# Linear attention feeding a two-layer MLP: four output tiles of block 0 held open beside batch 1's attention, and the steps of batches 2 and 3 moved

## The chip, the cores and the metric

The kernel runs on one core of a Trainium2 chip. The engines of the core are TensorE (PE in the profile, its weight loads PEld), VectorE (DVE), ScalarE (ACT), GpSimd (POOL) and SyncE (SP, which here only issues DMAs). The metric is the time of one execution on the device in microseconds, the median of several runs. Times inside a profile are microseconds from the start of its span.

## The reference

For 8 batches and 8 heads, with 576 tokens of 64 numbers, attention without a softmax is followed by a norm over each head; the heads are put side by side to 4608 tokens of 512 numbers, which go through two matrix products with a leaky rectifier between them.

```
kv  = einsum("bhsd,bhse->bhde", k, v)
o   = einsum("bhsd,bhde->bhse", q, kv)
o   = o / sqrt(mean(o*o, -1) + 1e-6) * g_norm
x   = o.transpose(0, 2, 1, 3).reshape(4608, 512)
h   = x @ w_in                                   # 4608 x 2048
g   = max(h, 0) + alpha * min(h, 0)
out = g @ w_out                                  # 4608 x 512, float32
```

## The kernel before

**Blocks and groups.** The 4608 tokens are cut into 9 blocks of 512 (`w`), so that blocks and batches of 576 tokens drift apart. For a block, the 2048 hidden numbers are 16 groups of 128 (`g`). `m1_group` (L480) makes one group: four matmuls of 512 columns over the four 128-row pieces of the input (L465), into one PSUM bank; ACT makes `m_sb` (L472), the rectified negative, and DVE puts both together to `gt` (L474), 128 x 512 in half precision. `y_mm` (L487) is one matmul of the second product: 128 tokens (tile `a`, four per block) by 512 outputs, with group `g` added in; 16 of them fill one output tile. `y_out` (L492) copies it out of PSUM on ACT or DVE, and SP issues two DMAs (L505). In the loop at L631 the output tiles of block `w - 1` are made beside the hidden groups of block `w`: in step `g`, after the group, four `y_mm` of tile `g // 4`.

**Attention.** Loads (L93) go through POOL's queue, two DMAs for each of q, k, v of a batch, from float32 into half precision. `regroup` (L105) copies q and k into another order, on DVE or POOL. Batches 0 and 1 (`NB_PE = 2`) are done with transposes on PE: `step_t` (L210) makes transposed q of a pair of heads, `step_kv` (L228) the product of k and v (20 matmuls, then a masking multiply on DVE, L242), `step_ot` (L262) the output of a pair for one block and its square, `ssq_mm` (L284) the sum of squares over a head by a matmul, with Ln and Exp on ACT, and `norm` (L295) the scaled input `xt` on DVE. The last 64 columns of batches 0 and 1 that fall in block 2 are the tail (L340, L352).

From batch 2 on, q is transposed by a DMA that SP issues (`transpose_q`, L376), and the attention goes by tiles of 128 tokens in four parts: `tile_a` (L384) product of q and kv into a bank and its square on ACT; `tile_b` (L397) the sum over each head on DVE (L399); `tile_c` (L405) Ln and Exp on ACT and the scale `rg` on POOL (L411); `tile_d` (L418) the scaled row `xrow` on DVE (L420) and one or two DMA transposes into `xm` (L425), the input of a block from block 2 on. `phase_steps(w)` (L431) lists for each step of block `w - 1` what is done for block `w`: a tile's `b` and `c` come one step after its `a`, its `d` two steps after.

**Order.** The order of the instructions on PE, ACT, DVE, POOL and SP is the program's: an instruction that waits holds those behind it on its engine. PSUM has eight banks: three for hidden groups (pool `psh`, tag `h`, taken in turn), one each for `y` and `s`, and `o0`, `o1`, `o2`.

**Around the change.** After block 0's groups (L579), three output tiles of block 0 (`ys`, L587) stay open while batch 1's attention runs; `ahead(g0, g1)` (L593) puts their `y_mm` of some groups between its steps, and L624 copies them out. The fourth tile is made in block 1's loop, one `y_mm` in each step (L638). In that loop the q of batch 2 is regrouped on DVE and transposed after step 1 (L655). After step 3 a one-element copy on POOL, `gate` (L662), waits for that transpose; behind it POOL issues the six loads of batch 3 (L663), and DVE regroups k of batch 2. After step 9 POOL regroups q and k of batch 3 (L665), and after step 13 SP issues its transpose. In block 2 and later the loads of batch `w + 2` are issued ahead of step 6 (L634). `KV_AT = 5` is the step of block 1 with batch 2's kv; its tiles start in step 7. In block 2, batch 3's kv is in step 0, and tiles start there too.

Of the kernel before, what the change touches and what calls it, by code (L numbers as in the profile page):

```python
# [9 lines left out]
FP32 = mybir.dt.float32  # L10
# [7 lines left out]
def kernel(  # L18
# [11 lines left out]
    nc = tc.nc  # L30
# [27 lines left out]
    ysb_p = ctx.enter_context(tc.tile_pool(name="ysb", bufs=4))  # L58
    ps_h = ctx.enter_context(tc.tile_pool(name="psh", bufs=3, space=bass.MemoryType.PSUM))
    ps_y = ctx.enter_context(tc.tile_pool(name="psy", bufs=1, space=bass.MemoryType.PSUM))  # L60
# [58 lines left out]
    for nm in "qkv":  # L119
        zero_rest(stages[0][nm])  # L120

    ident = const_p.tile([P, P], FP32, name="ident")
    make_identity(nc, ident[:])
    HH = H // 2
    for h0 in (0, HH):
        for nm in "qkv":
            load(0, nm, h0, h0 + HH)

# [204 lines left out]

    KV_AT = 5


# [93 lines left out]
    def phase_steps(w):  # L430
# [7 lines left out]
        steps = []  # L438
        kv_at = 0
        if w == NB_PE:  # L440
            n = NPAIR // JT
            for i in range(n + 1):
                m = [lambda i=i: step_tail_ot(i)] if i < n else []
                m += [lambda i=i: step_tail_ssq(i - 1)] if i > 0 else []
                steps.append(([], [], m))
            kv_at = KV_AT
            steps += [([], [], []) for i in range(KV_AT + 2 - len(steps))]
        for i in range(len(todo) + 2):
# [11 lines left out]

    gts = {}

    def m1_mm(h_ps, w, g, cs, cols=slice(0, W)):
# [15 lines left out]

    def m1_group(w, g, pool=(ps_h, "h")):  # L480
        h_ps = pool[0].tile([P, W], FP32, name="h_ps", tag=pool[1])
        m1_mm(h_ps, w, g, range(NC))
        m1_evac(h_ps, w, g)
# [34 lines left out]

    H_POOL = (ps_h, "h")
    O2 = (ps_o, "o2")  # L520
# [4 lines left out]
    )  # L525
    step_t(0, 0, H_POOL)
    step_t(0, 1, H_POOL, nc.scalar)
    regroup(0, "k", 0, HH)
# [7 lines left out]
    ssq_mm(0, 0)  # L536
    step_t(0, 2, H_POOL)
    step_t(0, 3, H_POOL)
    alpha_ps = ps_h.tile([P, NF], FP32, name="alpha_ps", tag="h")
    nc.tensor.matmul(  # L540
# [18 lines left out]
    half_ssq(0, O2)  # L559
    first = [ps_h.tile([P, W], FP32, name="h_ps", tag="h") for g in range(3)]  # L560
    first += [ps_o.tile([P, W], FP32, name="h_ps", tag=f"o{g}") for g in range(2)]
# [17 lines left out]
    for g in range(5, NF):  # L579
        m1_group(0, g, others.get(g, H_POOL))  # L580
        if g == 12:
            spread_g()

    AHEAD = 3
    ys = [  # L587
        ps_y.tile([P, W], FP32, name="ya", tag="y"),
        ps_o.tile([P, W], FP32, name="yb", tag="o0"),
        ps_o.tile([P, W], FP32, name="yc", tag="o1"),  # L590
    ]

    def ahead(g0, g1):  # L593
        for g in range(g0, g1):
            for a in range(AHEAD):
                y_mm(ys[a], 0, a, g)

    S_POOL = (ps_s, "s")
    regroup(1, "k")
    ahead(0, 4)  # L600
    regroup(1, "q")
    step_t(1, 0, S_POOL)
    step_t(1, 1, H_POOL, nc.scalar)
    step_t(1, 2, H_POOL)
    step_t(1, 3, H_POOL, nc.scalar)
    step_kv(1, pool=O2)
    step_ot(1, 0, S_POOL)
    step_ot(1, 1, H_POOL)
    step_ot(1, 2, H_POOL, nc.vector)
    step_ot(1, 3, H_POOL, nc.vector)  # L610
    ahead(4, 5)
    ssq_mm(1, 0)
    ahead(5, 7)
    ssq_mm(1, 1)
    norm(1, 0)
    ahead(7, 9)
    ssq_mm(1, 2)
    norm(1, 1)
    ahead(9, 11)
    ssq_mm(1, 3)  # L620
    norm(1, 2)
    norm(1, 3)
    ahead(11, NF)
    for a in range(AHEAD):  # L624
        y_out(ys[a], 0, a, nc.vector if a == 1 else None)
# [3 lines left out]

    LOAD_G = 6  # L630
    for w in range(1, NW):  # L631
        steps = phase_steps(w + 1)
        for g in range(NF):
# [4 lines left out]
            if w == 1:  # L638
                a, parts = AHEAD, [g]
            begin, mid, end = steps.pop(0) if steps else ([], [], [])  # L640
# [3 lines left out]
            for f in mid:  # L644
                f()
            if parts[0] == 0:
                pool, tag = ((ps_y, "y"), (ps_s, "s"))[a % 2 if w > 1 else 0]
                y = pool.tile([P, W], FP32, name="y_ps", tag=tag)
            for gg in parts:
                y_mm(y, w - 1, a, gg)  # L650
            if parts[-1] == NF - 1:
                y_out(y, w - 1, a)
            for f in end:
                f()
            if (w, g) == (1, 1):  # L655
                regroup(2, "q")
                transpose_q(2)
            if (w, g) == (1, 3):


                gate = const_p.tile([1, 1], FP16, name="gate")
                nc.gpsimd.tensor_copy(out=gate[:], in_=qtms[2][0:1, 0, 0:1])  # L662
                load_batch(3)  # L663
                regroup(2, "k")
            if g == LOAD_G + 3 and w + 2 < B:  # L665
                regroup_batch(w + 2)
            if g == NF - 3 and w + 2 < B:
                transpose_q(w + 2)
    for a in range(TPW):
        y = ps_h.tile([P, W], FP32, name="y_ps", tag="h")  # L670
        for g in range(NF):
            y_mm(y, NW - 1, a, g)
        y_out(y, NW - 1, a)
# [30 lines left out]
```

## Time and profile before

| what | value |
|---|---|
| median of 6 runs | 304.92 us (304.05 to 306.03) |
| the profiled execution's own time | 304.92 us |
| its span, first to last instruction | 302.9 us |
| PE busy | 284.6 us (94%), 1536 matmuls |
| DVE, ACT, POOL busy | 169.9, 152.9, 97.5 us |
| mean granted clock of PE | 0.987 of full speed |
| DMA queue of POOL (loads) / of SP (outputs, transposes) | 18.35 MB / 16.93 MB |
| block 1's first hidden group starts | 48.34 us |
| block 2's first hidden group starts | 78.32 us |

The page cuts the span into 40 slices and gives the busy share of each engine in tenths, and the clock that PE was granted. A line of the waits names the waiting engine, the tile and line, who released it, then microseconds in total, how often and the longest. A line of the timeline has start and duration, the engine, the line of code, the operation with its output and inputs, and in brackets how long the engine had been idle and who ended that. A matmul's shown duration (0.38 us) is longer than the spacing to the next (0.216 us), since they are pipelined. A DMA issue is listed with the time from issue to landing.

### The profile page before, as it was taken

The numbers are of one execution on the slowest core, as the hardware profiler recorded it, in microseconds if no ns is written. First come the engines' busy times: TensorE is split into PE (matmuls) and PEld (weight loads), VectorE is DVE, ScalarE is ACT, GpSimd is POOL, SyncE is SP. The second block draws the span as 40 slices with busy tenths as digits, with TensorE's granted clock in tenths as the row PEclk, the third lists the DMA queues.
The fourth block names the chain that finished last, engine by engine and source line by source line (L and its number), as shares of the span: only waits on it lengthen the run. The fifth ranks groups of instructions, "written<-read, shape, count | busy, mean of one in ns | idle before, by whom it ended". The sixth has DMA issues, their size and how long they took to land.

```text
span 302.9 us, 4249 instructions
## 1 busy us (share of the span) xinstructions
PE 284.6 (94%) x1536; PEld 137.6 (45%) x1536; DVE 169.9 (56%) x261; ACT 152.9 (50%) x297; POOL 97.5 (32%) x109
## 2 busy tenths in 40 slices
PE   5899999873999999999999999999999999999993
PEld 2554544431554454445544544454445444444441
DVE  5569765873486448545963584459546744344200
ACT  1558367460385448445844574458437644434220
POOL 9823400185047505560566054514002300000000
PEclk9999999998799999999999999999999999999999
DMA  7999999598619972994389739935211411122133
GB/s 95 184 206 202 202 203 229 131 163 126 121 33 128 209 169 45 152 230 98 69 112 214 146 78 123 241 80 89 61 35 37 95 35 37 35 47 54 41 69 69
DMA packets 66068, 35.54 MB, mean 117 GB/s; under 512 B 32752, under 2 KB 61440, under 8 KB 66048
## 3 DMA queue, kind: packets, MB, share of 16 engines
q0 software_dynamic: 29664, 18.35, 43.9%
q1 hardware_dynamic: 36384, 16.93, 26.6%
q8 instruction: 12, 0.20, 0.3%
q14 instruction: 8, 0.07, 0.1%
HBM read 36.71 MB, written 9.44 MB: 152 GB/s over the span
## 4 chain that ended last, share of the span: by engine, by line
PE 74%; DMA 11%; issue 8%; POOL 5%; DVE 0%; ACT 0%; POOLq 0%; ACTq 0%
PE y_ps L487 37%; PE h_ps L465 33%; DMA w_in_sb<-in_moe_w_in_dram 5%; DMA w_out_sb<-in_moe_w_out_dram 4%; DMA kst<-in_k_dram 3%; PE otm_ps L387 2%; PE kv_ps L238 2%; POOL w_in_sb L161 1%; POOL qst L96 1%; POOL vst L100 1%; POOL kst L96 1%; POOL qst L100 1%; POOL kst L100 0%; POOL vst L96 0%; POOL rg L411 0%
## 5 line engine op out<-in xcount | busy, mean ns | idle before, releaser
L474 DVE SCALAR_TENSOR_TENSOR gt<-m_sb,beta_sb,h_ps 128x512 f16<-128x512 f32 x144 | 105.8, 744 | 81.1 <-ACT m_sb L472 80.6
L487 PE MATMUL y_ps<-w_out_sb,gt 128*128 128x512 f16 x528 | 135.4, 380 | 0.0
L472 ACT ACTIVATE m_sb<-h_ps 128x512 f32<-128x512 f32 x144 | 85.5, 597 | 95.0 <-PE h_ps L465 94.4
L465 PE MATMUL h_ps<-xm,w_in_sb 128*128 128x512 f16 x448 | 115.7, 381 | 0.0
L465 PEld LDWEIGHTS <-w_in_sb 128*128 128x128 f16 x584 | 56.2, 99 | 69.6 <-issue 11.3
L487 PEld LDWEIGHTS <-gt 128*128 128x128 f16 x576 | 56.3, 98 | 66.8 <-issue 0.5
L411 POOL TENSOR_TENSOR rg<-ss,g_all 128x512 f32<-128x512 f32 (+1 forms) x30 | 31.3, 1046 | 83.7 <-ACT ss L409 83.7
L465 PE MATMUL h_ps<-xt,w_in_sb 128*128 128x512 f16 (+1 forms) x136 | 32.6, 381 | 7.2 <-DVE gt L474 7.2
L497 ACT COPY y_sb<-y_ps 128x512 f32<-128x512 f32 x33 | 19.2, 582 | 17.4 <-PE y_ps L487 17.1
L399 DVE TENSOR_REDUCE ss<-sqm_sb 128x8 f32<-128x512 f32 (+1 forms) x30 | 20.5, 683 | 9.4 <-ACT sqm_sb L393 9.3
L420 DVE TENSOR_TENSOR xrow<-otm_ps,rg 128x512 f16<-128x512 f32 (+1 forms) x30 | 20.4, 682 | 9.2 <-POOL rg L411 9.2
L393 ACT ACTIVATE sqm_sb<-otm_ps 128x512 f32<-128x512 f32 (+1 forms) x30 | 17.8, 592 | 8.5 <-PE otm_ps L387 8.5
L106 POOL COPY qsb<-qst 128x2560 f16<-128x2560 f16 x5 | 11.6, 2317 | 13.9 <-issue 10.2
L106 POOL COPY ksb<-kst 128x2560 f16<-128x2560 f16 x5 | 11.6, 2322 | 7.4 <-DMA kst<-in_k_dram 7.4
L387 PEld LDWEIGHTS <-qtm 128*128 128x128 f16 x120 | 9.2, 98 | 7.1
L197 PE MATMUL warm_ps<-warm,mask 128*128 128x512 f16 x26 | 8.7, 474 | 3.3 <-DVE eps_t L140 3.3
L387 PE MATMUL otm_ps<-kv_sb,qtm 128*128 128x128 f16 x120 | 11.6, 219 | 0.0
L406 ACT ACTIVATE ss<-ss,eps_t 128x8 f32<-128x8 f32 (+1 forms) x30 | 9.0, 301 | 4.7 <-DVE ss L399 4.6
L238 PE MATMUL kv_ps<-vst,ksb 128*128 128x128 f16 x160 | 10.4, 219 | 0.8 <-DMA vst<-in_v_dram 0.4
L238 PEld LDWEIGHTS <-ksb 128*128 128x128 f16 x160 | 9.5, 98 | 3.6 <-DVE ksb L106 1.7
L242 DVE TENSOR_TENSOR kv_sb<-kv_ps,mask 128x512 f16<-128x512 f32 (+1 forms) x9 | 5.7, 628 | 3.4 <-PE kv_ps L238 3.3
L100 POOL DMA_DIRECT2D vst<-in_v_dram x9 | 6.4, 716 | 3.3 <-DMA w_in_sb<-in_moe_w_in_dram 1.9
(72 smaller groups left out, 124.6 us busy)
## 6 DMA issues: line engine op xcount, KB each, us to landing
out_dram<-y_sb SPq DMA_DIRECT2D x72, 128.0 KB, 2.4
kst<-in_k_dram POOLq DMA_DIRECT2D x7, 320.0 KB, 8.2
qst<-in_q_dram POOLq DMA_DIRECT2D x7, 320.0 KB, 5.0
vst<-in_v_dram POOLq DMA_DIRECT2D x7, 320.0 KB, 10.7
w_in_sb<-in_moe_w_in_dram POOLq DMA_DIRECT2D x4, 512.0 KB, 10.5
w_out_sb<-in_moe_w_out_dram POOLq DMA_DIRECT2D x4, 512.0 KB, 15.5
kst<-in_k_dram POOLq DMA_DIRECT2D x7, 256.0 KB, 9.4
qst<-in_q_dram POOLq DMA_DIRECT2D x7, 256.0 KB, 6.4
```

What stands on the lines that cost most here:

```text
L106: (eng or nc.vector).tensor_copy(out=bufs[b % NBUF][nm][:, :, h0:h1, :].rearrange("p t h d -> p h t d"), in_=stages[b % NBUF][nm][:, h0:h1],)
L238: nc.tensor.matmul(out=kv_ps[:, j - j0, :], lhsT=ks(t), rhs=vs(t), start=(t == 0), stop=(t == NT - 1),)
L387: nc.tensor.matmul(out=ot_ps[:, 2 * j : 2 * j + 2, :], lhsT=qtms[b][:, t * NPAIR + j, :], rhs=kvs[b, j], start=True, stop=True,)
L393: nc.scalar.activation(out=sq[0:n], in_=ot_ps[0:n], func=AF.Square)
L399: nc.vector.tensor_reduce(out=ss[0:n], in_=sq[0:n], op=ALU.add, axis=mybir.AxisListType.X,)
L411: nc.gpsimd.tensor_tensor(out=rg[0:n], in0=ss[0:n].unsqueeze(2).to_broadcast([n, H, D]), in1=g_all[0:n].unsqueeze(1).to_broadcast([n, H, D ...
L420: nc.vector.tensor_mul(out=x[0:n], in0=ot_ps[0:n], in1=rg[0:n])
L465: nc.tensor.matmul(out=h_ps[:, cols], lhsT=w_in_blk(c, g), rhs=xt_of(w, c)[:, cols], start=(c == 0), stop=(c == NC - 1 and cols.stop == W),)
L472: nc.scalar.activation(out=m_sb[:], in_=h_ps[:], func=AF.Relu, scale=-1.0)
L474: nc.vector.scalar_tensor_tensor(out=gt[:], in0=m_sb[:], scalar=beta_sb[:, g : g + 1], in1=h_ps[:], op0=ALU.mult, op1=ALU.add,)
L487: nc.tensor.matmul(out=y[:], lhsT=gts[w, g][:, a * P : (a + 1) * P], rhs=w_out_blk(g), start=(g == 0), stop=(g == NF - 1),)
L497: nc.scalar.copy(out=y_sb[:], in_=y[:])
```

## The change

The three banks for hidden groups get a tag each (`h0`, `h1`, `h2`), and the code names the one that it takes; a counter turns them for the groups that name none. All four output tiles of block 0 are opened before batch 1's attention, in `h2`, `o0`, `o2` and `y`; the fourth runs to group 11 there, and groups 12 to 15 in the first four steps of block 1. Batch 1's attention uses `s`, `o1`, `h0` and `h1`; two pairs of `y_mm` stand around its kv; its fourth output comes later, after the first norm. The q of batch 2 is regrouped and transposed before block 0's outputs are copied out. Behind the gate only q and k of batch 3 are loaded, v after step 9; POOL's regroup moves from step 9 to 13 and the transpose of its q from step 13 to 15. In block 2 the steps for block 3 start two steps later, and kv of batch 3 moves from step 0 to step 3. At the start, the first half of batch 0's q is loaded ahead of the identity matrix.

```diff
+    HH = H // 2
+    load(0, "q", 0, HH)
     ident = const_p.tile([P, P], FP32, name="ident")
     make_identity(nc, ident[:])
-    HH = H // 2
     for h0 in (0, HH):
         for nm in "qkv":
-            load(0, nm, h0, h0 + HH)
+            if (h0, nm) != (0, "q"):
+                load(0, nm, h0, h0 + HH)
...
-        kv_at = 0
+        kv_at = {NB_PE: 5, NB_PE + 1: 3}.get(w, 0)
...
-            kv_at = KV_AT
-            steps += [([], [], []) for i in range(KV_AT + 2 - len(steps))]
+        n = {NB_PE: 7, NB_PE + 1: 2}.get(w, 0)
+        steps += [([], [], []) for i in range(n - len(steps))]
...
+    H_POOL = [(ps_h, f"h{i}") for i in range(3)]
...
+    n_group = [0]
+    def m1_group(w, g, pool=None):
+        if pool is None:
+            pool = H_POOL[n_group[0] % 3]
+            n_group[0] += 1
...
-    AHEAD = 3
+    LATER = 12
     ys = [
-        ps_y.tile([P, W], FP32, name="ya", tag="y"),
+        ps_h.tile([P, W], FP32, name="ya", tag="h2"),
         ps_o.tile([P, W], FP32, name="yb", tag="o0"),
-        ps_o.tile([P, W], FP32, name="yc", tag="o1"),
+        ps_o.tile([P, W], FP32, name="yc", tag="o2"),
+        ps_y.tile([P, W], FP32, name="yd", tag="y"),
     ]
-    def ahead(g0, g1):
+    def ahead(g0, g1, tiles=range(TPW)):
         for g in range(g0, g1):
-            for a in range(AHEAD):
-                y_mm(ys[a], 0, a, g)
+            for a in tiles:
+                if a < TPW - 1 or g < LATER:
+                    y_mm(ys[a], 0, a, g)
     S_POOL = (ps_s, "s")
+    O1 = (ps_o, "o1")
     regroup(1, "k")
-    ahead(0, 4)
+    ahead(0, 3)
     regroup(1, "q")
     step_t(1, 0, S_POOL)
-    step_t(1, 1, H_POOL, nc.scalar)
-    step_t(1, 2, H_POOL)
-    step_t(1, 3, H_POOL, nc.scalar)
-    step_kv(1, pool=O2)
-    step_ot(1, 0, S_POOL)
-    step_ot(1, 1, H_POOL)
-    step_ot(1, 2, H_POOL, nc.vector)
-    step_ot(1, 3, H_POOL, nc.vector)
+    step_t(1, 1, O1, nc.scalar)
+    step_t(1, 2, H_POOL[0])
+    step_t(1, 3, H_POOL[1], nc.scalar)
+    ahead(3, 4, range(2))
+    step_kv(1, pool=S_POOL)
+    ahead(3, 4, range(2, TPW))
+    step_ot(1, 0, O1)
+    step_ot(1, 1, H_POOL[0])
+    step_ot(1, 2, H_POOL[1], nc.vector)
     ahead(4, 5)
-    ssq_mm(1, 0)
+    ssq_mm(1, 0, S_POOL)
     ahead(5, 7)
-    ssq_mm(1, 1)
+    ssq_mm(1, 1, S_POOL)
     norm(1, 0)
-    ahead(7, 9)
-    ssq_mm(1, 2)
+    ahead(7, 8)
+    step_ot(1, 3, O1, nc.vector)
     norm(1, 1)
+    ahead(8, 9)
+    ssq_mm(1, 2, S_POOL)
     ahead(9, 11)
-    ssq_mm(1, 3)
+    ssq_mm(1, 3, S_POOL)
     norm(1, 2)
+    ahead(11, NF)
     norm(1, 3)
-    ahead(11, NF)
-    for a in range(AHEAD):
+    regroup(2, "q")
+    transpose_q(2)
+    for a in range(TPW - 1):
         y_out(ys[a], 0, a, nc.vector if a == 1 else None)
...
             if w == 1:
-                a, parts = AHEAD, [g]
+                a, y = TPW - 1, ys[TPW - 1]
+                parts = [LATER + g] if LATER + g < NF else []
...
-            if (w, g) == (1, 1):
-                regroup(2, "q")
-                transpose_q(2)
             if (w, g) == (1, 3):
                 gate = const_p.tile([1, 1], FP16, name="gate")
                 nc.gpsimd.tensor_copy(out=gate[:], in_=qtms[2][0:1, 0, 0:1])
-                load_batch(3)
+                load(3, "q")
+                load(3, "k")
                 regroup(2, "k")
-            if g == LOAD_G + 3 and w + 2 < B:
+            if (w, g) == (1, 9):
+                load(3, "v")
+            if g == (13 if w == 1 else LOAD_G + 3) and w + 2 < B:
                 regroup_batch(w + 2)
-            if g == NF - 3 and w + 2 < B:
+            if g == (15 if w == 1 else NF - 3) and w + 2 < B:
                 transpose_q(w + 2)
```

## The prediction

> **What bounds the kernel now.** I read four views in this order: the 40 slices of the page, TensorE's waits, the timeline around the slices that are not full, and the landing times of the DMA issues there. The slices first:
>
> ```profile
> PE   5899999873999999999999999999999999999993
> ...
> PEclk9999999998799999999999999999999999999999
> ```
>
> A slice is 7.6 us. TensorE (PE) is full except at the start and in slices 8 to 11, about 53 to 83 us, where its clock falls too. From 82 us to the last output PE runs back to back, so time can come only from PE's idle and slow time before that. The list of PE's waits (total, times, longest):
>
> ```profile
> PE h_ps L465 <- DVE gt L474: 7.2, 4, 4.8
> ...
> PE ot_ps L271 <- DVE kv_sb L242: 0.8, 1, 0.8
> ```
>
> Four waits for a hidden bank to be emptied by VectorE (DVE) make 7.2 us: 0.43, 1.35, 0.61 and 4.85 us, all in block 1 (w = 1). The timeline of the engines that lead to the longest:
>
> ```profile
> 59.08 0.18 POOL L662 COPY gate<-qtm 1x1 f16<-1x1 f16 x1 [19.04 <-DMA qtm<-qsb]
> ...
> 66.73 2.32 POOL L106 COPY qsb<-qst 128x2560 f16<-128x2560 f16 x1 [1.00 <-DMA qst<-in_q_dram]
> ...
> 69.35 2.32 POOL L106 COPY ksb<-kst 128x2560 f16<-128x2560 f16 x1 [0.30 <-DMA kst<-in_k_dram]
> ...
> 71.63 1.04 POOL L411 TENSOR_TENSOR rg<-ss,g_all 128x512 f32<-128x512 f32 x1
> 72.71 0.69 DVE L420 TENSOR_TENSOR xrow<-otm_ps,rg 128x512 f16<-128x512 f32 x1 [4.74 <-POOL rg L411]
> ...
> 74.11 1.86 PE L465 MATMUL h_ps<-xt,w_in_sb 128*128 128x512 f16 x4 [4.85 <-DVE gt L474]
> ```
>
> The reader sees one chain: GpSimd (POOL) stands in the regroup copies of batch 3, whose data were asked for only at 59.57, after the gate; the scale rg of tile (2,2) is queued behind them; xrow of that tile holds DVE; the gts behind xrow hold PE's banks. The price goes on after the wait (columns: busy time of PE, PEld, DVE, ACT, POOL, then clock):
>
> ```profile
> 72.00:73.00 1.00, 0.00 (x0) 0.00 (x0) 0.29 (x1) 0.00 (x0) 0.67 (x1) 1.00 0.89 89
> 73.00:74.00 1.00, 0.00 (x0) 0.00 (x0) 1.00 (x3) 0.00 (x0) 0.00 (x0) 0.53 0.03 5
> ...
> 79.00:80.00 1.00, 1.00 (x4) 0.34 (x3) 0.52 (x1) 0.21 (x1) 0.00 (x0) 0.56 0.04 6
> 80.00:81.00 1.00, 1.00 (x20) 1.00 (x19) 0.21 (x1) 0.60 (x1) 0.00 (x0) 1.00 0.56 127
> ```
>
> The granted clock halves 3.8 us after PE went idle (69.26) and is back at about 79.9. Between 74.11 and 79.96 PE does 14 matmuls of 512 columns; at the full-clock spacing of 0.216 us they take 3.02, so the slow clock costs 2.83 us, 0.77 of it after block 2 begins at 78.32 (3.84 us until its group 1 at 82.16, for 0.86 + 1.12 + 0.86 + 0.23 = 3.07 of work).
>
> **The change, part by part.** I set the time at which block 2's first hidden group starts (78.32 now) against the same point after. Rows used: h group of 4 matmuls 0.86; y matmul 0.216; 20 matmuls of kv or a transposed q 1.11; tile's product 0.23; last matmul's start to its reader 0.42; ACT m_sb 0.60 (next one after 0.48); DVE gt 0.75 (next after 0.65), reduce 0.68, xrow 0.69; POOL rg 1.04, one load issue 0.68.
>
> *Batch 1's attention.* PE stands at 32.21 in both. Twelve y matmuls run to 34.80; PE waits for the regrouped q at 35.48 as now; transposes to 36.59. New: two y matmuls, then kv to 38.11, two more y, and PE waits for kv_sb (multiplied 1.33 us after kv's start, 0.69 long) until 39.10 instead of 38.85; 0.5 us of PE's pause remains. Outputs 0 to 2 end at 39.77. Bank s now serves kv and all four sums of squares in turn; the readers are done in time (Ln of pair 0 ends at 41.73, the next sum comes at 42.58; then 43.68 before 44.75, and 45.85 before 46.70). Output 3 waits for bank o1 until norm 0 ends at 43.17 and comes at 43.66; its square is ready at 45.52, before its sum at 46.70. So no wait is added. With 60 y matmuls for 48, block 1 starts at 50.37 (now 48.34): 2.59 us of work came forward, 0.56 of pause was filled. If the w_out quarters were late this would fail: they land at 39.1, 41.6 and 45.1, and are used at 39.8, 43.9 and 47.8.
>
> *q of batch 2 and its transpose* go before the outputs. It lands at 46.4 and 47.7, so DVE copies it at 49.14 to 49.96 behind norm 3 without waiting. Behind it on DVE is the copy of ya's neighbour yb (to 51.05), needed by the tail product at 51.23: covered by 0.2 us. On SP the transpose (3.2 us) passes ahead of the six output issues, which nobody waits for soon (four buffers). The transpose itself is issued at 50.0, beside batch 2's loads, which land until 54.6. Quiet it takes 4.9 us; the one issued at 104.07 beside loads took 6.3 and landed 2.7 after them. I take 57.4; bounds 54.9 and 58. Tile (2,0) wants it at 60.27.
>
> *Block 1.* Groups start at 50.37, 51.68, 52.98, 54.06, 55.14, 56.08: y matmuls only in the first four, tail in the first two. DVE's k copy of batch 2 follows gt 3 and ends at 57.41, so kv in step 5 waits 0.52 us (0.38 now). Groups 6 to 11: 58.55, 59.41, 60.50, 61.58, 62.67, 63.53. So at group 11 PE is level with now (63.58). From here the tiles set the pace, through a loop of reduce, Ln, Exp, next square: 1.78 us a tile (60.95 to 62.73 now), against 1.09 for a group. Reduces at 61.8, 63.5, 65.4. POOL is not waiting on loads any more: gate 57.4, four issues (q, k) until 60.6; rg (2,0) at 63.1, (2,1) at 64.9. Then the two v issues, 1.37 us, stand before rg (2,2): 67.3 to 68.35, a delay of 0.6. xrow (2,2) at 68.45, gt 11 at 69.06. PE's groups 12, 13, 14 wait for gts 9, 10, 11: 65.6, 67.5, 69.85, three waits of 1.2, 1.0 and 1.5. Group 15 ends at 71.57.
>
> *Block 2's start* also needs the third xm transpose, issued at 69.1 behind xrow. Bounds:
>
> ```profile
> xm<-xrow SPq DMA_TRANSPOSE x1, 7.9
> ```
> ```profile
> xm<-xrow SPq DMA_TRANSPOSE x1, 2.4
> ```
>
> The first is the one issued at 65.49 amid batch 3's loads, the second the one issued at 73.4 in quiet; the one at 67.3 took 6.5. Here only v is in flight, issued at 65.9 and 66.6; at the 200 GB/s of the loads its 576 KB take 2.9 us, so traffic ends near 71. Landing between 71.5 and 75.6; I take 72.5, nearer the quiet row. **Block 2 starts at 72.5 instead of 78.32: 5.8 us earlier**, and the clock's tail of 0.77 goes.
>
> The Trainium skill, "DMA: Bandwidth & Descriptors", section "Queues, rings and completion order", says that each DMA engine takes turns between its queues packet by packet. By that a transpose beside loads would about double, and land near 73.9; the 7.9 row says more than turns, so the row is kept as the far end.
>
> *Steps of batch 3 in block 2.* The steps move back by two, kv from step 0 to 3. POOL regroups q and k behind rg (2,2), to 73.0; q's transpose lands near 76, v near 72; kv is at about 79, tile (3,0) at about 81: covered by 5 us. But batch 4's six load issues at step 6 (4.1 us of POOL) now stand before rg of tiles (3,1) and (3,2), which today are done. With S5 the start of step 5: rg (3,0) ends at S5 + 3.3, loads to + 7.5, rg (3,1) to + 8.5, its xrow and then gt 7 to + 9.9; PE's group 10 wants that bank at + 9.1. A new wait of 0.85 (bounds 0 and 3.2, the whole delay of rg). Their xm transposes still have some 6 us before block 3.
>
> *q before the identity:* POOL issues the first q pair 0.7 us earlier, the rest when it did. PE is in its warm-up until 7.47 anyway: nothing; bounds 0 and a gain of 0.7. The tags of banks are the same rotation: nothing, as in the last outputs.
>
> **Sum:** 5.8 + 0.77 - 0.85 = 5.7 us off the profiled execution's 304.92 (span 302.9 and 2.0 around it), which is also the median: **299.2 us**.
>
> **Rivals.**
> 1. *The clock falls in block 1.* Between 66.4 and 69.85 PE would be busy for 0.86 of 3.4 us. For: it halved at 73.0. Against: between 64.82 and 68.02 it was busy for 0.86 of 3.2 us (waits 1.35 and 0.61) and the clock stayed at 1.00. Price as now, 2.83 + 0.77 = 3.6: 302.8 us.
> The Trainium skill, "TensorE: Matmul & The Clock Gate", section "A second HAM failure mode: psum-queue depth-cycling", speaks against this change: short idles between matmul groups that cycle through banks make the clock swing. By it the sum would be 302.8; by the row of 64.82 to 68.02, 299.2; I follow the row.
> 2. *The last xm transpose lands with the slow rows (slower than before).* At 69.1 + 6.5 = 75.6 PE is idle from 71.57 for 4.0 us, past the 3.8 at which the clock fell: 3.1 more wait and 3.6 of slow clock, 305.9 us. It decides from a landing at 75.4. For: two rows of 6.5 and 7.9. Against: those had six loads in flight until 73.4, this has two.
> 3. *The tiles flow better.* If v's issues don't delay rg, the transpose lands quiet, q's early load helps by 0.7 and step 6 costs nothing: 71.6 less 0.6, 296.5 us.
> 4. *The change doesn't do what it says:* the gate comes late (q's transpose starved until about 62), k and v land later and POOL's copies again hold back step 3 and 4 of block 2, a wait like today's but shorter, some 4 us: 303.2 us.
>
> **How the numbers follow.** Forecast with its neighbourhood 0.70; rival 1 0.12; rival 2 0.05; rival 3 0.08; rival 4 0.05. Range 296.5 to 302.8: from rival 3 to rival 1. A measurement of this kernel tells 0.3% (0.9 us) from no change: faster, below 304.0, holds all but rival 2 and part of 4: 0.92; same 0.03; slower 0.05.
>
> **What would show it.** Right: PE's longest wait in block 1 falls from 4.85 to under 2 us, the clock stays at 1.00 around 73 to 80, no regroup of batch 3 stands before the third rg, the gate is near 57, block 1 starts near 50.4 and block 2 near 72.5, and a wait of about 1 us appears at group 10 of block 2. Wrong: a slow clock before 80, a wait of h_ps for xm over 2 us, or a wait for q's or kv's operands in block 2.

## The result, and the profile after

The changed kernel took 302.33 us (median of 28 runs, 300.87 to 304.67; a 29th, 305.57 us, over 1.5% above the fastest, is not counted), the kernel before 304.48 us (65 runs, 303.22 to 306.03): ratio 0.994, 95% interval 0.9927 to 0.9953. So it is faster, by 2.15 us. The forecast was 5.7 us faster: the sign and the range held, the size did not. The profiled execution took 303.55 us (span 301.5); in the time of its own profile it gained 1.37 us.

The slices of the page of after:

```profile
PE   5799999974999999999999999999999999999993
...
PEclk9999999999799999999999999999999999999999
```

Counted from 1, the dip of PE is now two slices, 9 and 10 (60 to 75 us); before it was three, 8 to 10. The clock still falls once, in slice 11. PE's waits in after (total, times, longest):

```profile
PE h_ps L467 <- DVE gt L476: 4.2, 4, 1.6
...
PE h_ps L467 <- DMA xm<-xrow: 2.5, 1, 2.5
PE kv_ps L240 <- DMA vst<-in_v_dram: 1.2, 1, 1.2
```

The wait of 4.85 us for a bank is gone, and the same list has a new line: 2.5 us for the transpose xm. (The wait for v is batch 0's, at 11.17 us.) The timeline of after (start, duration, engine, operation, idle time before it and what ended that) shows how the chain runs now:

```profile
56.56 0.18 POOL L675 COPY gate<-qtm 1x1 f16<-1x1 f16 x1 [15.52 <-DMA qtm<-qsb]
...
66.78 0.74 POOL L96 DMA_DIRECT2D vst<-in_v_dram  x1 [0.21 <-issue]
67.51 0.70 POOL L100 DMA_DIRECT2D vst<-in_v_dram  x1
...
68.20 1.07 POOL L411 TENSOR_TENSOR rg<-ss,g_all 128x512 f32<-128x512 f32 x1
69.19 2.34 POOL L106 COPY qsb<-qst 128x2560 f16<-128x2560 f16 x1
69.30 0.69 DVE L420 TENSOR_TENSOR xrow<-otm_ps,rg 128x512 f16<-128x512 f32 x1 [1.28 <-POOL rg L411]
70.70 1.89 PE L467 MATMUL h_ps<-xt,w_in_sb 128*128 128x512 f16 x8 [1.61 <-DVE gt L476]
75.14 1.25 PE L467 MATMUL h_ps<-xm,w_in_sb 128*128 128x512 f16 x4 [2.54 <-DMA xm<-xrow]
```

The gate opens at 56.56 instead of 59.08. No regroup copy stands before the third rg any more (the q copy follows it, at 69.19), only v's two issues. xrow, which held everything at 72.71 before, is at 69.30. But its transpose, issued at 70.0, lands at 75.0, and PE, done with block 1 at 72.6, stands until 75.14. The times from issue to landing of v's two loads (issued at 66.78 and 67.51) and of that transpose:

```profile
vst<-in_v_dram POOLq DMA_DIRECT2D x1, 320.0 KB, 4.9
vst<-in_v_dram POOLq DMA_DIRECT2D x1, 256.0 KB, 7.1
```
```profile
xm<-xrow SPq DMA_TRANSPOSE x1, 5.0
```

So v landed at 71.7 and 74.6. What the wait does to the clock is in the windows of after (columns: busy time of PE, PEld, DVE, ACT, POOL, then the granted clock):

```profile
72.00:74.00 2.00, 0.59 (x3) 0.09 (x1) 1.49 (x2) 0.96 (x2) 1.78 (x1) 1.00 1.78 153
74.00:76.00 2.00, 0.86 (x4) 0.44 (x5) 0.01 (x1) 0.00 (x0) 0.00 (x0) 0.95 1.08 236
76.00:78.00 2.00, 2.00 (x6) 0.69 (x5) 0.75 (x1) 0.60 (x1) 0.00 (x0) 0.50 0.41 91
78.00:80.00 2.00, 2.00 (x8) 0.75 (x7) 0.00 (x0) 0.39 (x1) 0.00 (x0) 0.70 0.00 0
```

The clock halves shortly before 76 and is back at about 79.2. The first two groups of block 2 with their y matmuls (16 matmuls at 0.216 us, 3.46 us) take from 75.14 to 80.27, 5.13 us: 1.67 us lost, where the tail before lost 0.77. Further on, in block 2 of after:

```profile
94.68 2.11 POOL L411 TENSOR_TENSOR rg<-ss,g_all 128x512 f32<-128x512 f32 x2
...
97.23 1.02 PE L467 MATMUL h_ps<-xm,w_in_sb 128*128 128x512 f16 x4 [0.75 <-DVE gt L476]
```

The six loads of batch 4 (90.59 to 94.7) hold two rg, and PE waits 0.75 us for the bank: the new wait that was forecast.

The account within the profile: block 2 starts 3.18 us earlier (75.14 for 78.32), the clock takes 0.90 more (1.67 for 0.77), the new wait 0.75: 1.53 us, and the spans differ by 1.4.

### The profile page after: what moved, and what is told of

Same layout as the page of the kernel before. It is cut to its first block, busy times and chain, and to the rows that moved or that the text cites. A ratio compares the mean times of both kernels' runs of the same rounds, so it can differ in the third digit from the quotient of the medians.

```text
span 301.5 us, 4250 instructions
## 1 busy us (share of the span) xinstructions
PE 283.4 (94%) x1536; PEld 136.8 (45%) x1536; DVE 169.0 (56%) x261; ACT 152.9 (51%) x297; POOL 98.5 (33%) x109
## 4 chain that ended last, share of the span: by engine, by line
PE 82%; DVE 5%; DMA 4%; POOL 4%; issue 2%; ACT 2%; POOLq 0%; ACTq 0%
PE h_ps L467 37%; PE y_ps L494 35%; PE kv_ps L240 3%; DMA vst<-in_v_dram 2%; DVE gt L476 2%; PE otm_ps L387 2%; DMA xm<-xrow 2%; POOL rg L411 1%; PE yb L494 1%; PE ya L494 1%; DVE xrow L420 1%; PE yc L494 1%; DVE ss L399 1%; PE yd L494 1%; POOL vst L96 1%
## 5 line engine op out<-in xcount | busy, mean ns | idle before, releaser
L494 PE MATMUL y_ps<-w_out_sb,gt 128*128 128x512 f16 x512 | 129.7, 381 | 0.0
L467 PE MATMUL h_ps<-xt,w_in_sb 128*128 128x512 f16 (+1 forms) x136 | 30.3, 366 | 3.5 <-DVE gt L476 3.5
L96 POOL DMA_DIRECT2D qst<-in_q_dram x9 | 7.0, 779 | 3.2 <-DVE g_all L523 2.0
```

Of the source, the lines that this page charges most:

```text
L467: nc.tensor.matmul(out=h_ps[:, cols], lhsT=w_in_blk(c, g), rhs=xt_of(w, c)[:, cols], start=(c == 0), stop=(c == NC - 1 and cols.stop == W),)
L494: nc.tensor.matmul(out=y[:], lhsT=gts[w, g][:, a * P : (a + 1) * P], rhs=w_out_blk(g), start=(g == 0), stop=(g == NF - 1),)
```

## The experiments

Three theories. **L** (landing): the third xm transpose lands late because v's loads are in flight beside it. **C** (clock): a clock that falls in some executions takes the gain. **T** (tile): the fourth open tile itself costs time, since it takes filler work out of the end of block 1, where PE waits for the attention tiles. Ratios are to the kernel before, with 95% intervals; edits are on after unless it is said otherwise.

### Which part gives the gain

**e7_place_only**: the kernel before with only the new places of batch 3's steps.

```diff
...
-                load_batch(3)
+                load(3, "q")
+                load(3, "k")
...
+            if (w, g) == (1, 9):
+                load(3, "v")
-            if g == LOAD_G + 3 and w + 2 < B:
+            if g == (13 if w == 1 else LOAD_G + 3) and w + 2 < B:
-            if g == NF - 3 and w + 2 < B:
+            if g == (15 if w == 1 else NF - 3) and w + 2 < B:
```

> The kernel before with only the new places of the steps for batch 3: v after step 9, GpSimd's regroup after step 13, the transpose of q after step 15, block 2's steps two later and kv in its step 3. Three output tiles stay open as before, the fourth is made step by step in block 1, and q of batch 2 is transposed after step 1. If block 1 is paced by the chain of tiles, the work that the fourth open tile brings forward buys nothing, and this kernel gives what the whole change gives: 301.5 to 303. If the open tile earns its own share (up to 2.6 us of work out of block 1), this one stays at 303.5 or more.

304.09 us, ratio 0.9987 [0.9964, 1.0011]: no difference. The gate stays late (60.6 us), PE waits 3.5 us for xm, block 2 starts at 76.65, and the clock falls. This is the number that was expected if the open tile earns its share; e8 and e13 show that this reading is wrong.

**e8_tile_only**: the kernel before with only the fourth tile and the tags of banks; batch 3's steps and q of batch 2 as before.

```diff
...
-    for a in range(AHEAD):
+    for a in range(TPW - 1):
...
-                a, parts = AHEAD, [g]
+                a, y = TPW - 1, ys[TPW - 1]
+                parts = [LATER + g] if LATER + g < NF else []
```

> The changed kernel with only the fourth open tile and the banks' tags: the start, batch 2's q after step 1, all loads of batch 3 at the gate, its regroup after step 9 and block 2's steps are as before. If the places of the steps are what counts, the long wait behind GpSimd's regroup is still there and block 1 only starts 2 us later with 2.6 us less in it: 303.5 to 305.5. If the open tile earns its share, up to 2.5 us less than before: 302.

305.54 us, ratio 1.0029 [1.001, 1.0049]: slower. Its timeline shows the chain of before, one step further on:

```profile
70.72 2.32 POOL L106 COPY ksb<-kst 128x2560 f16<-128x2560 f16 x1 [0.77 <-DMA kst<-in_k_dram]
73.00 1.04 POOL L408 TENSOR_TENSOR rg<-ss,g_all 128x512 f32<-128x512 f32 x1
...
75.47 3.15 PE L464 MATMUL h_ps<-xt,w_in_sb 128*128 128x512 f16 x7 [3.97 <-DVE gt L473]
```

PE's waits for gt grow from 7.2 to 8.2 us, and block 2 starts at 78.84. The tile brings nothing alone.

**e13_no_tile**: the kernel before with the new places and with q of batch 2 regrouped and transposed ahead of block 0's outputs; three open tiles, old order of the first loads.

```diff
...
+    regroup(2, "q")
+    transpose_q(2)
...
-            if (w, g) == (1, 1):
-                regroup(2, "q")
-                transpose_q(2)
...
```

> The kernel before with the new places for batch 3's steps and the early regroup and transpose of batch 2's q, but three open output tiles and the fourth made in block 1: the whole change but the open tile and the start. If the early transpose, which opens the gate 4 us earlier, is what the places alone lacked, 301.5 to 302.5, as the whole change; the open tile then earns nothing. If the open tile earns its share, 303.5 or more.

300.11 us, ratio 0.987 [0.9842, 0.9898]: 2.2 us better than the whole change, and lower than either outcome that was expected. The early transpose of q is what the places needed: e7 lacks only it and takes 4.0 us more by the medians, 2.3 more between the runs of both with a mean clock of 0.998 or above (302.39 and 300.05). PE's waits in block 1 and the start of block 2:

```profile
66.11 1.02 PE L466 MATMUL h_ps<-xt,w_in_sb 128*128 128x512 f16 x4 [0.61 <-DVE gt L475]
...
68.74 1.02 PE L466 MATMUL h_ps<-xt,w_in_sb 128*128 128x512 f16 x4 [1.39 <-DVE gt L475]
...
72.70 1.02 PE L466 MATMUL h_ps<-xm,w_in_sb 128*128 128x512 f16 x4 [1.64 <-DMA xm<-xrow]
```

Block 1 starts at 48.57 here and at 50.97 in after; block 2 at 72.70 and 75.14. PE does the same work up to block 2 but for the tile's 12 y matmuls, 2.59 us, which now run inside block 1, in waits that PE has there anyway: its waits for banks in block 1 and for xm before block 2 are 3.6 us (0.61 + 1.39 + 1.64) against 6.0 in after (1.02 + 0.83 + 1.61 + 2.54).

### The landing of the transpose

**e2_v_late**: v of batch 3 is loaded two steps later.

```diff
-            if (w, g) == (1, 9):
+            if (w, g) == (1, 11):
```

> The changed kernel with v of batch 3 loaded after step 11 of block 1 instead of after step 9, so that its two issues stand behind the last scale rg, and its transfers begin behind the last transposes. Theory A, the transposes are held by v's loads: the third transpose lands within about 3 us of its issue instead of 5.0, block 2 starts near 72 instead of 75.1 us, the clock stays at full speed, and the time falls by 3.5 to 4.5 us, to about 298.3. Theory B, they are held by what is late anyway (the output writes of block 0 that now follow batch 2's transpose, and k of batch 3 behind them, which landed at 69.1): the landing and the wait of 2.5 us stay, and the time falls by less than 1 us, the 0.6 to 1.0 by which rg comes earlier.

304.46 us, ratio 1.0002 [0.998, 1.0024]: the whole gain is lost. The edit did not part loads and transposes: POOL issued v at 68.2 and 68.9, right behind rg (2,2), and SP its transpose at 68.7. Earlier than in after, and yet it landed no earlier: at 75.0, as v did (75.2). It took 6.3 us; the transpose before it, issued at 66.9 ahead of v, took 2.6. PE waited 3.8 us for it and the clock fell to 0.50.

**e5_v_with_k**: v goes with q and k, at the gate.

```diff
-                load(3, "q")
-                load(3, "k")
+                load_batch(3)
```

> The changed kernel with v of batch 3 loaded behind its q and k at the gate again, no longer after step 9: the split alone undone. In every run so far the third transpose landed with the last load of v (75.0 beside 74.6, 75.0 beside 75.1, 74.3 beside 73.8), also where it was issued first. Theory A, transposes make no headway until the loads beside them are done: from the gate at 56.6 the six loads take 13.8 us as before, so they end near 71 and the third transpose lands at 71 to 72 instead of 75; block 2 starts 2.5 to 3.5 us earlier, the clock stays, and the time is 298 to 299.5. Theory B, the output writes hold the transposes: no change, 302.3. Theory C, the chain of tiles is the bound and GpSimd's two more issues ahead of the first scale delay it: up to 1 us slower.

301.2 us (12 runs), ratio 0.9914 [0.9889, 0.994]. The last load lands at 73.1 (12.3 us after its issue), the third transpose at 74.6; PE still waits 3.1 us for it. 298 to 299.5 was expected. An earlier issue alone does not get v out of the transposes' way: behind q and k it took longer to land.

**e6_v_gated**: v is asked for only when the third xm transpose has landed, by a second one-element copy on POOL.

```diff
-            if (w, g) == (1, 9):
+            if (w, g) == (1, 13):
+                regroup(3, "q", eng=nc.gpsimd)
+                gate_v = const_p.tile([1, 1], FP16, name="gate_v")
+                nc.gpsimd.tensor_copy(out=gate_v[:], in_=xm(2)[0:1, 0, W - 1 : W])
                 load(3, "v")
...
```

> The changed kernel with v of batch 3 held by a second one-element copy on GpSimd that waits for the third transpose of block 2's input, behind the regroup of q: loads of v and the transposes can't meet. Theory A: the third transpose lands 2.4 to 3 us after its issue, at about 72; the clock stays; but v is asked for at about 72.5 and lands near 78, so its kv in step 3 of block 2 waits up to 2 us: 299 to 301. Theory B: the transposes still take 5 us or more without any load of v in flight, and the time is 303 or more.

300.27 us, ratio 0.9868 [0.984, 0.9896]: 2.06 us better than after. The third transpose of e6, issued at 68.5, with its time to landing, and PE's timeline:

```profile
xm<-xrow SPq DMA_TRANSPOSE x1, 2.4
```
```profile
71.81 1.03 PE L467 MATMUL h_ps<-xm,w_in_sb 128*128 128x512 f16 x4
...
79.71 1.28 PE L240 MATMUL kv_ps<-vst,ksb 128*128 128x128 f16 x20 [1.47 <-DMA vst<-in_v_dram]
```

2.4 us instead of 5.0; no wait for xm is left, and block 2 starts 3.33 us earlier than in after (0.68 of it because block 0's output tiles start at 32.27 and not at 32.95). This decides for L. The other suspect in the expectations, the output writes of block 0, is out as well: in after the last of them landed at 67.5, before the third transpose was issued. A part is given back: kv in step 3 now waits 1.47 us for v.

This profile also shows a clock at 0.50 from 67.6 to 71.0, in block 1. It costs less there than at the start of block 2: from block 1's first group to block 2's it takes 21.51 us (50.30 to 71.81), and 20.79 us (50.99 to 71.78) in the next kernel, whose clock stayed at 1.00. So 0.7 us are lost; the next kernel stands 0.80 us for the bank of group 14, this one does not, so that a part of the slow clock is hidden in that wait.

**e15_gated_kv4**: e6 with batch 3's kv a step later, to hide that wait.

```diff
-        kv_at = {NB_PE: 5, NB_PE + 1: 3}.get(w, 0)
+        kv_at = {NB_PE: 5, NB_PE + 1: 4}.get(w, 0)
```

> The changed kernel with v of batch 3 gated by the third transpose, and its kv in step 4 of block 2. From the gated run's 300.3 its wait of 1.5 us for v goes: 298.8 to 299.2, which is what was forecast for the change with a transpose that lands soon. If v is still late, 299.5 or more.

300.03 us, ratio 0.9842 [0.9816, 0.9869], not apart from e6; 298.8 to 299.2 was expected. The wait was exchanged: v's is 0.25 us, but kv now holds bank s when the next output tile wants it.

```profile
82.91 1.02 PE L494 MATMUL y_ps<-w_out_sb,gt 128*128 128x512 f16 x4 [1.23 <-DVE kv_sb L244]
```

### The clock

**e12_fill**: ten matmuls of constants, read by nobody, between block 1 and block 2, so that PE is not idle in the last wait.

```diff
+            if (w, g) == (1, 15):
+                idle_ps = ps_s.tile([P, W], FP32, name="idle_ps", tag="s")
+                for i in range(10):
+                    nc.tensor.matmul(
+                        out=idle_ps[:], lhsT=mask16[:], rhs=warm16[:], start=True, stop=True,
+                    )
```

> The changed kernel with ten matmuls added on TensorE after step 15 of block 1, of constants into a free bank and read by nobody: 2.2 us of work inside the wait of 2.5 us for the transpose. If the slow clock of block 2's first steps is a price of that wait, it goes: 1.3 to 1.7 us less in the runs that have it, a median near 301.5 and no run above 303. If the clock falls for another reason, 302.3 or more.

302.84 us, ratio 0.9943 [0.9918, 0.9968]. Nine runs in two groups: four whose mean granted clock was 0.998 or 0.999 took 301.63 to 302.02, five at 0.987 to 0.991 took 302.84 to 304.14. The profile is of the second kind, and its windows show why the fill came too late:

```profile
66.00:68.00 2.00, 1.02 (x4) 0.39 (x4) 2.00 (x5) 1.58 (x6) 1.58 (x2) 1.00 1.39 192
68.00:70.00 2.00, 1.25 (x4) 0.47 (x4) 0.71 (x3) 1.00 (x3) 2.00 (x4) 0.71 1.14 100
70.00:72.00 2.00, 1.17 (x4) 0.33 (x3) 2.00 (x4) 0.60 (x1) 2.00 (x1) 0.50 1.31 195
```

The clock fell at 69, between groups 12 to 14, and stayed low until 75.7, so that a part of the added matmuls ran slowly too; block 2 starts at 77.38. In after's profile PE is as idle there (busy 1.02 of 2 us in each of the two windows from 66 to 70) and the clock stays at 1.00. So the last wait is not the only place where it can fall.

**e14_fill_all**: the same, with three such matmuls after each of the steps 11 to 14 and eight after step 15.

```diff
+            if w == 1 and g > 10:
...
+                for i in range(8 if g == 15 else 3):
```

> The changed kernel with matmuls of constants, read by nobody, added at the ends of steps 11 to 14 of block 1 (three each) and 15 (eight): inside all four waits for hidden banks and for the transpose, 4.3 us of work. In two profiled runs the clock fell at 68 to 70 us, before the last wait, and filling that one alone did not keep it. If the slow clock comes from TensorE's small share of work between 65 and 75 us as a whole, it stays at full speed now and all runs lie near the faster ones of the changed kernel: 301.3 to 302, none above 303. If the added work delays the groups, 302.3 or more.

301.53 us, ratio 0.9898 [0.9864, 0.9932]; all four runs at a clock of 0.996 or more, none above 302.73. Block 2 starts at 74.95, as late as in after: a kept clock does not bring the transpose.

**e4_own_outputs**: work that counts in the same place. The 12 y matmuls of block 1's own first output tile, 2.59 us, are done in steps 12 to 15.

```diff
...
+    OWN = {12: range(0, 4), 13: range(4, 8), 14: range(8, 10), 15: range(10, 12)}
...
+                own = OWN.get(g, [])
...
+            for gg in own if w == 1 else []:
+                y_mm(y_own, 1, 0, gg)
...
```

> The changed kernel with twelve output matmuls of block 1's own first tile put into steps 12 to 15 of block 1, and block 2's output matmuls three steps earlier for it: the same work, put where TensorE waits. If the waits there (1.0, 0.8, 1.6 and 2.5 us) are TensorE's alone and the clock falls because of them, 2.6 us of work is hidden in them and the slow clock at block 2's start (1.7 us) goes: about 4 us less, 298.3. If the clock falls from the last wait alone, it still falls (idle about 2 us): 2 to 2.6 us less, 300. If the waits grow because the chain of tiles is delayed by the added work, less than 1 us.

299.81 us (299.0 to 300.14), ratio 0.9849 [0.9823, 0.9875], clock 0.997 to 0.999 in all four runs. PE's wait for xm is 1.3 us. It is 2.5 us better than after: the waits of block 1 hold the work that the fourth tile had taken out of them.

### The start, and batch 4

**e1_q_order**: the first q is loaded in its old place.

```diff
-    load(0, "q", 0, HH)
...
-            if (h0, nm) != (0, "q"):
-                load(0, nm, h0, h0 + HH)
+            load(0, nm, h0, h0 + HH)
```

> The changed kernel with the first half of batch 0's q loaded behind the identity matrix again, as before; all else as changed. In the changed kernel's trace the first kv waits 1.2 us for v and block 0's output tiles start at 32.95 instead of 32.21 us. If the moved load is the cause (k's and v's first issues came 0.4 us later and landed up to 1.2 us later), the start point goes back to about 32.2 and the time falls by about 0.7 us, to 301.6. If the start of the loads only varies from one execution to the next, the start point may lie anywhere and the median stays at 302.3.

301.48 us, ratio 0.9916 [0.9883, 0.9949], which holds after's 0.994: not told apart. In the profiles block 0's output tiles start at 31.4 to 32.8 with the old order (seven kernels, mean 32.1) and at 32.1 to 33.4 with the new one (eleven, mean 32.6). The early load gains nothing; whether it costs half a microsecond stays open.

**e3_loads_split**: batch 4's loads are spread over steps 6 and 7 of block 2.

```diff
-            if g == LOAD_G and 3 < w + 2 < B:
+            if g == LOAD_G and 3 < w + 2 < B and w > 2:
...
+            if (w, g) == (2, 6):
+                load(4, "q")
+            if (w, g) == (2, 7):
+                load(4, "k")
+                load(4, "v")
```

> The changed kernel with batch 4's loads in block 2 issued behind the scales of the last two tiles: q after step 6, k and v after step 7, instead of all six ahead of step 6. If the six issues hold up rg and through it the hidden bank of group 10, the idle of 0.75 us near 95 us goes and the time falls by 0.7 us, to 301.6. If that idle has another cause, it stays. A new wait for k of batch 4 at block 3's start, about 2 us less in hand, would show that the issues were early for a reason.

302.33 us, ratio 0.994 [0.9916, 0.9964], as after. The wait at group 10 is gone, and another of the same kind comes one block on:

```profile
109.75 1.28 PE L240 MATMUL kv_ps<-vst,ksb 128*128 128x128 f16 x20 [1.13 <-DMA vst<-in_v_dram]
```

### Put together

**e10_own_gated**: e4 and e6 in one, with kv in step 4. **e11_own_gated_v4**: e10 with v of batch 4 one step later.

```diff
...
-                load_batch(w + 2)
+                for nm in "qk" if w == 2 else "qkv":
+                    load(w + 2, nm)
...
+            if (w, g) == (2, 7):
+                load(4, "v")
...
```

> The changed kernel with three edits together: twelve output matmuls of block 1's first tile in its steps 12 to 15, v of batch 3 gated by the third transpose, and kv of batch 3 in step 4 of block 2 instead of 3. From the gated run's 300.3: its wait of 1.5 us for v goes with the later kv, and the three waits of 2.6 us for hidden banks take 2.6 us of work: 296 to 297.5. If the added work lies on the chain of tiles, or v still comes late, 298 to 299.

> The same with v of batch 4 issued after step 7 of block 2, its q and k ahead of step 6 as before: GpSimd's stay ahead of the last two scales falls from six issues to four. If the idle of 0.75 us near 95 us comes from these issues, 0.4 to 0.7 us less than the run beside it; if v of batch 4 is then late for block 3, as in the run where k and v both came later, no gain.

e10 took 296.97 us, ratio 0.9757 [0.9736, 0.9778], clock 0.997 or more in each run; e11 297.38 us, 0.9768 [0.9746, 0.9789]. L and the filler add up (0.994 to 0.9868 and to 0.9849 alone); batch 4's wait is only exchanged, as in e3 (0.60 us at group 10 in e10, 0.70 us ahead of batch 4's kv in e11, whose v landed at 102.1).

**e16_notile_gated**: e13 with v gated and kv in step 4, so e15 without the fourth tile (and with the old order of the first loads). **e17_notile_own_gated**: e16 with block 1's own outputs in steps 12 to 15, as in e4. The edit of e16 against e13, in part:

```diff
...
     regroup(2, "q")
     transpose_q(2)
...
-        kv_at = {NB_PE: 5, NB_PE + 1: 3}.get(w, 0)
+        kv_at = {NB_PE: 5, NB_PE + 1: 4}.get(w, 0)
...
+                nc.gpsimd.tensor_copy(out=gate_v[:], in_=xm(2)[0:1, 0, W - 1 : W])
...
```

> The same two edits on the kernel without the fourth open tile (three open tiles, steps placed as changed, early transpose of batch 2's q). If the open tile costs time because block 1 starts 2 us later and its chain of tiles with it, this kernel is 1.5 to 2.2 us below the run beside it: 296.8 to 297.5. If the open tile only hurt through where the transposes met the loads, both are alike: 298.8 to 299.2.

> As the run before, with twelve output matmuls of block 1's own first tile in its steps 12 to 15. The best run so far, with four open tiles, gave 296.97. If the work of the fourth tile is worth most as filling of block 1, and more filling from block 1 itself still finds waits (about 1.5 us are left), 295 to 296.3. If the waits are used up by then, as the run before, 296.5 to 297.5.

e16: 298.4 us, ratio 0.9806 [0.9774, 0.9838], 1.6 us below e15. From the start of block 0's output tiles to block 2 it takes 37.90 us, e15 39.06: 1.16 us are the tile's own; the other half microsecond may be the start. Two of its six runs lie 1.5 and 2.1 us above the other four at the same clock (0.999), which nothing here explains. **e17 is the best kernel: 295.66 us, ratio 0.9707 [0.9678, 0.9735]**, four to five times the gain of the change (the median gap to e10 is 1.3 us). Its clock, and PE's waits for v and for hidden banks in the whole span:

```profile
PEclk9999999999999999999999999999999999999999
```
```profile
PE kv_ps L238 <- DMA vst<-in_v_dram: 0.8, 2, 0.5
...
PE h_ps L466 <- DVE gt L475: 0.6, 1, 0.6
```

Of 7.2 us of waits for gt before, none is left in block 1: the 0.6 is at 91.29, in block 2, and the waits for v are batch 0's and 1's, at 9.54 and 36.31. The list has no wait for xm.

## Why the prediction was right about the chain and wrong in its sum

| step | forecast | measured in after |
|---|---|---|
| block 1 starts after the output tiles | 18.16 us | 18.02 us (from 32.95; forecast from 32.21) |
| gate | 57.4 | 56.56 |
| kv in step 5 waits | 0.52 | 0.38 |
| groups 12, 13, 14 wait | 1.2, 1.0, 1.5 | 1.02, 0.83, 1.61 |
| third transpose issued | 69.1 | 70.0 |
| it lands | 72.5 (71.5 to 75.6) | 75.0 |
| block 2 starts | 72.5 | 75.14 |
| the clock against before | 0.77 gained | 0.90 lost |
| wait at group 10 of block 2 | 0.85 | 0.75 |

The mechanism was right: the wait of 4.85 us went, and the groups of block 1 (counted from the start of block 0's output tiles), the waits that replace it and the new one in block 2 came within 0.25 us of their forecasts. But two of the prediction's own signs of being wrong came too: a slow clock before 80 us and a wait for xm of over 2 us. Two terms of the sum failed, and they account for the miss. In the profiled execution, 303.55 - 299.2 = 4.35 us: block 2 2.64 late, the clock 1.67, the wait at group 10 0.10 better, together 4.21.

**The landing of the third xm transpose (mis-sized term).** "I take 72.5, nearer the quiet row" was the step that failed. Of 2.64 us, 0.9 is the later issue (0.74 of it the later start of block 0's output tiles in this execution; e6, with the same code up to there, starts them at 32.27). 1.6 us is the landing itself, 5.0 instead of 3.4 us, and 0.14 lies between landing and start. I had let v's traffic end near 71, by its bytes over the mean rate; by the prediction's own numbers (66.6 and 2.9) that is 69.5, and the rest up to 71 has no source. v landed at 71.7 and 74.6: in the windows of 2 us from 68, 70 and 72 us the DMAs moved 95, 210 and 153 GB/s, the transposes included, and not 200 for v alone. The second and third transposes landed at 74.4 and 75.0, with v, so the slow rows of before were the right neighbours, as rival 2 had it. The reason against them, six loads in flight, said too much: when those two were issued (65.49 and 67.34), one and two of the six had landed. e6 shows the quiet case: 2.4 us, block 2 at 71.81.

The Trainium skill, "DMA: Bandwidth & Descriptors", section "Queues, rings and completion order", says that each DMA engine takes turns between its queues packet by packet; the prediction's estimate from it, about twice the quiet time, was not used in its sum. For this transpose it was nearer than the forecast: from the measured issue at 70.0, twice 2.4 us gives 74.8, and it landed at 75.0. As a rule for this case it is too mild: the second transpose of after took 7.0 us, the third of e2 6.3, the first of before 7.9.

**The clock (rival 1).** It was given 0.12. One profile shows the late landing without the fall: e1 has the same waits for banks as after (1.02, 0.83 and 1.61 us), but its clock stays at 1.00 from 66 to 76 us. Block 2 starts at the same time:

```profile
75.03 1.02 PE L464 MATMUL h_ps<-xm,w_in_sb 128*128 128x512 f16 x4 [1.98 <-DMA xm<-xrow]
```

That execution took 301.74 us, 1.81 less than after's; block 2's start is 0.11 of it, and the clock's 1.67 nearly all the rest. In five of the 28 runs of after the mean granted clock was 0.998 or 0.999, with a median of 301.96 us; in fifteen it was 0.992 to 0.994, with 303.56: 1.6 us, close to the 1.67 of the trace. The mean is a rough sign, since it holds the end of the span too (e13's profile is at 1.00 until 294 us, its last 3.4 us at 0.60, and its mean is 0.995): three of the fifteen took only 301.28 to 301.88. The other runs are seven at 0.984 or 0.985, which took no longer (median 301.76), and one at 0.981 with 304.30. I have no trace of the seven; a fall during block 1's waits would be cheap, as the one in e6, but that they fell there is not shown. So rival 1 was right that the clock can fall in spite of the row of 64.82 to 68.02. That row was misread: the windows give 1.25 us of work in its 3.2 us, not 0.86, for the step's output matmul was left out. In after's profile the fall came later than rival 1 had it, after PE's 2.54 us of waiting for xm; so the 3.8 us of idle time ahead of the fall in before were no bound. That this last wait alone made the clock fall is not shown: e12 fills it, and the clock fell in five of nine runs. What kept the clock in every run is work in the waits of block 1 and the last one (e14, e4). Against the median of all runs the clock is a small part: the runs that kept it lie only 0.4 us below the median, and 2.8 us above the forecast.

Rival 1's price of 3.6 counts 0.77 twice, since 2.83 holds it already: by its own rows it is 2.83, and the upper end of the range would be 302.0. That the range held at 302.33 is luck in this respect. The terms of rival 3 add up to 296.2, not 296.5.

The Trainium skill, "TensorE: Matmul & The Clock Gate", section "What's actually happening", says that the window by which the clock is judged, about 3.4 us, runs freely, and that the point at which the clock changes at a kernel's start therefore varies. Carried over to a fall in mid-kernel, this would let it depend on where the idle time lies in the window. That agrees with e12, whose runs split into two groups, and with the same waits at 66 to 70 us that cost the clock in e12's profile and not in after's and e1's; no run here places the windows on purpose. Its section "A second HAM failure mode: psum-queue depth-cycling", which the prediction had weighed and set aside, was nearer the truth than my single row: in e12 the clock falls between groups that each wait about 1 us (1.02, 0.83 and 0.83).

**The fourth tile (not asked).** The prediction counted 2.59 us of work brought forward and 0.56 us of pause filled, and derived block 1's waits rightly from the tile chain. It did not draw the conclusion: with the chain as the bound, the chain starts later by what was put ahead of it, and steps 12 to 15 are left without filler. e13, e16 and e17 show the price: 2.2, 1.6 and 1.3 us against the same kernels with the tile, of which half a microsecond by the profiles' starting points, or 0.85 by the medians of after and e1, which are not told apart, may be the order of the first loads. So theory T holds beside L; C is real, but against the median a small part of the miss.

**q's early load** was put between nothing and a gain of 0.7; no gain is seen. The prediction had q's first issue 0.7 us earlier and the rest unmoved. In after it is 0.2 us earlier (1.25 for 1.45) and k's 0.36 later (3.20 for 2.84).

## What to carry to other kernels

In these runs, work that can go anywhere belonged in the stage that another engine's chain paces, not ahead of it: there it was nearly free, and it kept the clock up. When loads are brought forward, ask which later small transfers they will meet, and let the loads wait for the landing of those (a one-element copy is enough) instead of placing them by their own due times. Undo each part of a change alone: here one part (the tile, with the order of the first loads) cost 2.2 us, about half of what another (the early transpose) gave.

## What the runs showed of the hardware

- The third xm transpose, from SBUF to SBUF on SP's queue, took 2.4 us alone (e6). Issued beside POOL's loads of v it landed with the last of them or up to 1.5 us later (e5: 73.1 and 74.6), even when it was issued before part of them: in e2 issued at 68.7 and landed at 75.0, v issued at 68.2 and 68.9 and landed by 75.2. It is no rule for every transpose: the first of after, issued at 65.55, landed at 69.8 with k (69.1), ahead of v (71.7 and 74.6).
- The granted clock differs between executions of one kernel (mean 0.981 to 0.999 in after), and between profiles with the same waits for banks (after and e1). In the profiles a fall lasted 3.4 us (after, e2, e5, e6, e7) or two or three times that (6.8 in before and e12, 10.2 in e3 and e8). A fall cost about 1.6 to 1.9 us where its tail reached block 2 (medians of the groups: after 303.56 and 301.96; e5 302.72 and 301.11; e7 304.25 and 302.39), and 0.7 us in the start of block 2 where it ended in block 1 (e6 against e15).
- A load asked for earlier need not come earlier: the first q's regroup began at 5.56 to 5.68 us with the old order in all profiles but one (6.36), and at 6.26 to 6.33 with the new one, where its load was issued 0.2 us earlier.
